# Attention sums in one PSUM bank: half-width matmuls for the left-over queries

## The chip, the cores and the metric

The kernel runs on one core of a Trainium2 chip. A core has TensorE (PE, matrix products into PSUM), VectorE (DVE), ScalarE (ACT), GpSimd (POOL), SyncE (SP, here only issuing transfers), 16 DMA engines, an on-chip memory of 128 partitions (SBUF) and the accumulator memory PSUM with eight banks of 2 KiB per partition. The metric is the device time of one execution in microseconds.

## The reference

An attention over 8 batches of 12 heads, with normalized queries and keys, followed by a feed-forward layer over all 3584 rows.

```python
batch, n_heads, seq, head_dim = (8, 12, 448, 64)
def rmsnorm(x, g):
    rms = np.sqrt(np.mean(x * x, axis=-1, keepdims=True) + 1e-06)
    return x / rms * g
q_n, k_n = (rmsnorm(q, g_q), rmsnorm(k, g_k))
scores = scale * np.matmul(q_n, k_n.transpose(0, 1, 3, 2))
scores = scores - np.max(scores, axis=-1, keepdims=True)
attn = np.exp(scores)
attn = attn / (np.sum(attn, axis=-1, keepdims=True) + 1e-09)
attn_out = np.matmul(attn, v)
...
x = attn_out.transpose(0, 2, 1, 3).reshape(B * S, H * D)      # 3584 x 768
h = x @ w_in                                                  # 768 -> 2048
relu6 = np.clip(h + 3.0, 0.0, 6.0)
out = (h * relu6 / 6.0) @ w_out                               # 2048 -> 768
```

## The kernel before

**Pairs of heads.** Two heads make a pair (48 pairs, six a batch), and one pair's 128 columns are one contraction block of the feed-forward. The 448 positions of a head are three blocks of 128 and a rest of 64 (`NT` = 3, `REST` = 64). The two rests of the keys share one 128-row block with zeros elsewhere, so that a fourth key block serves both heads at once.

**What is done for a pair `p`.** Keys, queries and values are loaded as fp32. `square` (POOL, early also ACT), `sums` (DVE) and `rstd` (two small ACT instructions) give the inverse root of the mean square; `normalize` (POOL, one instruction for keys and one for queries) writes bf16. Eight 128x128 blocks are then transposed, by PE into PSUM for the first 16 pairs (`transposes`, line 384) and by a DMA transpose afterwards; `put_q` scales the queries with the gains. `score` (line 407) multiplies keys by queries: for the three full key blocks one matmul per head, each on 64 rows of the array, the two heads' matmuls writing to two banks; for the rest block a single one of 128 rows. `expo` (line 417, ACT) writes the exponentials as bf16 tiles `eD` (both heads) or `eR` (rest block), laid out key by query.

**The weighted sums.** `weigh` (line 430) uses a window of 128 query columns of an exponential tile as weights and the value block with an added column of ones (`vaug`, 64 + 1 columns) as moving data, so that the output has queries on partitions and the denominator in its 65th column. 448 queries do not fill four windows. The exponential tiles are therefore 512 columns wide (`W4`), and columns 448 to 511 are filled once with ones by `fill_e`. In even batches the fourth window is 384 to 511; in odd batches the windows are shifted so that the 64 left-over queries stand on partitions 64 to 127, where the joint row blocks of two batches want them. Each key block gives eight matmuls of 65 columns, the rest block four of 130. The sums of a pair lie in `av`, four windows at a stride of 256 fp32, that is two banks. `divide` (lines 438 and 439, DVE) takes the reciprocal of the denominators and multiplies, giving `xn`. `x_out` (line 449, PE, first 12 pairs, then copied by `put_x`) or a DMA transpose (`x_out_dma`) turns `xn` into `xT`, the moving operand of the feed-forward.

**The feed-forward.** For each batch, `h_mm` (line 463) makes 16 groups of six matmuls with 448 columns; `relu` (line 469, ACT) and `gate` (line 474, DVE) turn each into a block of `gT`. `y_mm` (line 482) makes 16 matmuls of 384 columns for each half of an output row block, `y_copy` copies them out, `y_store` writes the rows. Weights come over POOL's DMA queue.

**PSUM.** Two double banks (`sc`, for scores), two single banks (`ps`) and the two of `av`: eight. Feed-forward groups use the single banks, `ff_banks`, and, after the last score, the double ones too.

**What sets the order.** No scheduler of a library does: the class `Plan` (lines 45 to 222) plays the kernel through at build time with estimated costs in ns and writes the instructions of every engine in the order in which its model starts them. Each `add(key, ways, deps, ...)` is a step, with the engines that can take it, its cost, and a rank. For PE, feed-forward groups (`item`) and attention steps share the engine by `share`, a credit per unit of batch progress. `PRICE` and `FIRST` weigh one engine against another, `BULK`, `LATE`, `SLACK` describe transfers, `CALM` holds the weight loads back while other transfers are queued (line 187), `NFAST` is the number of first pairs whose squares may go to ACT, and `ANY` the order in which banks are tried. At run time engines only wait for each other's semaphores; the order is fixed.

Of the kernel before, what the change touches and what calls it, by code (L numbers as in the profile page):

```python
# [44 lines left out]
class Plan:  # L45
# [3 lines left out]
    PRICE, FIRST, UNTIL = {"POOL": 0.5, "ACT": 2.0, "DVE": 1.5}, {"POOL": 0.7, "ACT": 1.5, "DVE": 0.9}, 45e3  # L49
# [122 lines left out]
    def run(self):  # L172
        now = 0.0
        while self.todo or self.row or any(self.lanes.values()):
# [8 lines left out]
            for op in self.known:  # L183
# [3 lines left out]
                if op.calm is not None and (self.backlog("SP", "ACT") > op.calm[0] or self.backlog("POOL") > op.calm[1]):  # L187
                    continue
# [37 lines left out]
def kernel(  # L226
# [48 lines left out]
    ssq_r = ring(NR, [P, 2, 8], FP32, "ssq")  # L275
    lnv_r = ring(NR, [P, 2, 8], FP32, "lnv")
    rstd_r = ring(NR, [P, 2, 8], FP32, "rstd")
# [4 lines left out]
    rden_r = ring(2, [P, 4, 2], FP32, "rden")  # L282
    xn_r = ring(NQ, [P, 4, 2 * D], BF16, "xn")
# [6 lines left out]
    unit_r = ring(2, [P, 2, 512], FP32, "sc", psum) + ring(2, [P, 1, 512], FP32, "ps", psum)  # L290
    av_ps = psum.tile([P, 4, 256], FP32, name="av")
# [7 lines left out]
    plan = Plan(share=(1.0, 1.0, 0.45, 3.0, 0.42, 6.0, 0.4))  # L299
# [57 lines left out]
    def sums(p, a, m):  # L357
        nc.vector.tensor_reduce(  # L358
            out=ssq_r[p % NR][:, a].rearrange("p a s -> p (a s)"),
            in_=sq_r[m % 2][:, a].rearrange("p a s d -> p (a s) d"), axis=mybir.AxisListType.X, op=A_ADD,  # L360
        )

    def rstd(p, a):
        nc.scalar.activation(out=lnv_r[p % NR][:, a], in_=ssq_r[p % NR][:, a], func=LN, bias=1e-6, scale=1.0 / D)
        nc.scalar.activation(out=rstd_r[p % NR][:, a], in_=lnv_r[p % NR][:, a], func=EXP, bias=0.0, scale=-0.5)  # L365

    def normalize(eng, p, a):
        eng.tensor_tensor(  # L368
            out=qkn_r[p % NQ][:, a].rearrange("p t h d -> p h t d"), in0=qk_st[:, a, p % NS],
            in1=rstd_r[p % NR][:, a].rearrange("p (h t) -> p h t", h=2).unsqueeze(3).to_broadcast([P, 2, 4, D]),  # L370
# [481 lines left out]
```

## Time and profile before

| what | value |
|---|---|
| median of 3 runs | 429.16 us (429.08 to 430.69) |
| the profiled execution | 428.99 us |
| its span, first to last instruction | 427.2 us |
| granted TensorE clock | 0.999 |
| busy: PE, ACT, DVE, POOL | 407.9, 264.7, 219.3, 213.5 us |
| first matmul | 8.83 us |
| last weighted sum (`av`) | 325.9 us |

The profile is of one execution. Its page lists busy time by engine, forty slices of the span, DMA queues, the chain of work that ended last, and groups of instructions by line and shape; the trace behind it answers for stretches and single instructions. Busy time of PE counts every matmul from its first read to its modelled end, so neighbours overlap and the busy share says little of the rate; the rate is the distance of starts. "PEld" rows are the loading of weights, which overlaps matmuls. A shape such as `64*128 64x448` is that of the weights' array part and of the moving data.

### The profile page before, as it was taken

The numbers are of one execution on the slowest core, as the hardware profiler recorded it, in microseconds if no ns is written. First come the engines' busy times: TensorE is split into PE (matmuls) and PEld (weight loads), VectorE is DVE, ScalarE is ACT, GpSimd is POOL, SyncE is SP. The second block draws the span as 40 slices with busy tenths as digits, with TensorE's granted clock in tenths as the row PEclk, the third lists the DMA queues.
The fourth block names the chain that finished last, engine by engine and source line by source line (L and its number), as shares of the span: only waits on it lengthen the run. The fifth ranks groups of instructions, "written<-read, shape, count | busy, mean of one in ns | idle before, by whom it ended". The sixth has DMA issues, their size and how long they took to land.

```text
span 427.2 us, 8968 instructions
## 1 busy us (share of the span) xinstructions
PE 407.9 (95%) x3536; PEld 232.4 (54%) x3536; DVE 219.3 (51%) x382; ACT 264.7 (62%) x490; POOL 213.5 (50%) x233
## 2 busy tenths in 40 slices
PE   1888999999999999999999999999999999999997
PEld 0555555555555455555555555555566555555565
DVE  5686867674553756556556465324344253253222
ACT  4998888778677888778776787567751142032100
POOL 6999989884594779868858377301000000000000
PEclk9999999999999999999999999999999999999999
DMA  7999998999999999999698858343202200100122
GB/s 198 233 253 217 163 226 142 237 179 198 220 243 268 194 227 185 250 226 216 133 272 170 191 130 176 61 111 76 64 12 75 75 0 38 74 2 37 73 76 74
DMA packets 125738, 64.03 MB, mean 150 GB/s; under 512 B 74736, under 2 KB 122240, under 8 KB 125696
## 3 DMA queue, kind: packets, MB, share of 16 engines
q1 hardware_dynamic: 114480, 56.72, 59.5%
q0 software_dynamic: 10528, 6.31, 11.0%
q8 instruction: 27, 0.44, 0.5%
q10 hardware_dynamic: 688, 0.43, 0.3%
q14 instruction: 15, 0.12, 0.1%
HBM read 45.61 MB, written 11.01 MB: 133 GB/s over the span
## 4 chain that ended last, share of the span: by engine, by line
PE 83%; POOL 4%; DMA 3%; ACT 3%; DVE 2%; SPq 2%; issue 2%; ACTq 0%; POOLq 0%
PE ps L482 32%; PE ps L463 29%; PE av L430 8%; PE sc L407 8%; PE sc L482 3%; DMA qk_st<-in_q_dram 2%; PE sc L463 2%; POOL sq L355 2%; ACT eD L417 1%; POOL qkn L368 1%; SPq L332 1%; DVE ssq L358 1%; DMA v_st<-in_v_dram 1%; DVE gT L474 1%; SPq L324 1%
## 5 line engine op out<-in xcount | busy, mean ns | idle before, releaser
L463 PE MATMUL ps<-xT,w_in_sb 128*128 128x448 bf16 x720 | 163.8, 353 | 1.1 <-DVE gT L474 0.9
L482 PE MATMUL ps<-w_out_sb,gT 128*128 128x384 bf16 (+1 forms) x832 | 151.7, 323 | 0.1
L417 ACT ACTIVATE eD<-sc 128x896 bf16<-128x896 f32 x144 | 127.5, 915 | 22.1 <-PE sc L407 14.2
L469 ACT ACTIVATE t_sb<-ps 128x448 f32<-128x448 f32 x120 | 65.4, 545 | 77.3 <-PE ps L463 73.6
L482 PEld LDWEIGHTS <-gT 128*128 128x128 bf16 x912 | 83.2, 98 | 55.0 <-issue 8.1
L474 DVE SCALAR_TENSOR_TENSOR gT<-t_sb,ps 128x448 bf16<-128x448 f32 x120 | 74.1, 618 | 75.2 <-ACT t_sb L469 74.7
L368 POOL TENSOR_TENSOR qkn<-qk_st,rstd 128x512 bf16<-128x512 f32 x96 | 97.9, 1043 | 24.8 <-ACT rstd L365 22.0
L463 PEld LDWEIGHTS <-w_in_sb 128*128 128x128 bf16 x768 | 68.4, 97 | 60.5 <-issue 12.8
L355 POOL TENSOR_TENSOR sq<-qk_st 128x1024 f32<-128x1024 f32 (+1 forms) x46 | 82.1, 1799 | 8.8 <-DMA qk_st<-in_q_dram 6.7
L407 PE MATMUL sc<-qkT 64*128 64x448 bf16 (+1 forms) x336 | 60.7, 359 | 4.8 <-ACT eD L417 3.4
L358 DVE TENSOR_REDUCE ssq<-sq 128x16 f32<-128x1024 f32 (+1 forms) x50 | 58.4, 1171 | 11.3 <-POOL sq L355 7.1
L430 PEld LDWEIGHTS <-eD 128*128 128x128 bf16 x1152 | 53.0, 98 | 20.4 <-issue 3.1
L335 DVE COPY y_sb<-ps 128x384 f32<-128x384 f32 (+1 forms) x45 | 24.7, 548 | 68.6 <-PE ps L482 68.5
L430 PE MATMUL av<-vaug,eD 128*128 128x65 bf16 x1152 | 58.7, 194 | 0.0
L335 POOL CAST vaug<-v_st 128x512 bf16<-128x512 f32 x32 | 19.7, 619 | 55.7 <-PE av L430 54.8
L417 ACT ACTIVATE eR<-sc 128x448 bf16<-128x448 f32 x48 | 26.1, 544 | 12.9 <-PE sc L407 12.6
L439 DVE TENSOR_TENSOR xn<-av,rden 128x512 bf16<-128x512 f32 x48 | 33.2, 691 | 1.7
L407 PEld LDWEIGHTS <-qkT 64*128 64x128 bf16 (+1 forms) x336 | 14.9, 94 | 32.9 <-issue 27.4
L438 DVE RECIPROCAL rden<-av 128x8 f32<-128x8 f32 x48 | 9.8, 205 | 27.3 <-PE av L430 26.7
L396 ACT ACTIVATE qkT<-qkT,gprime 128x448 bf16<-128x448 bf16 x32 | 21.4, 668 | 1.0 <-DMA qkT<-qkn 1.0
L430 PE MATMUL av<-vaug,eR 128*128 128x130 bf16 x192 | 19.0, 222 | 0.3 <-DVE xn L439 0.3
L430 PEld LDWEIGHTS <-eR 128*128 128x128 bf16 x192 | 14.0, 98 | 8.5 <-issue 1.9
(54 smaller groups left out, 146.7 us busy)
## 6 DMA issues: line engine op xcount, KB each, us to landing
v_st<-in_v_dram SPq DMA_DIRECT2D x24, 384.0 KB, 6.0
qk_st<-in_k_dram SPq DMA_DIRECT2D x23, 384.0 KB, 4.6
qk_st<-in_q_dram SPq DMA_DIRECT2D x23, 384.0 KB, 5.1
out_dram<-y_sb SPq DMA_DIRECT2D x23, 384.0 KB, 2.6
w_in_sb<-in_moe_w_in_dram POOLq DMA_DIRECT2D x8, 384.0 KB, 5.8
w_out_sb<-in_moe_w_out_dram POOLq DMA_DIRECT2D x4, 768.0 KB, 10.9
out_dram<-y_sb SPq DMA_DIRECT2D x9, 192.0 KB, 2.7
v_st<-in_v_dram SPq DMA_DIRECT2D x24, 64.0 KB, 5.1
```

What stands on the lines that cost most here:

```text
L335: (eng.copy if eng is nc.scalar else eng.tensor_copy)(out=out, in_=in_)
L355: eng.tensor_tensor(out=sq, in0=x, in1=x, op=A_MULT)
L358: nc.vector.tensor_reduce(out=ssq_r[p % NR][:, a].rearrange("p a s -> p (a s)"), in_=sq_r[m % 2][:, a].rearrange("p a s d -> p (a s) d"), ...
L368: eng.tensor_tensor(out=qkn_r[p % NQ][:, a].rearrange("p t h d -> p h t d"), in0=qk_st[:, a, p % NS], in1=rstd_r[p % NR][:, a].rearrange(" ...
L407: nc.tensor.matmul(out=bank(u, h)[:, 0:S], lhsT=qkT[rows, 0, i * P:(i + 1) * P], rhs=qkT[rows, 1, 0:S], start=True, stop=True,)
L417: nc.scalar.activation(out=e[..., 0:S], in_=src[..., 0:S], func=EXP, bias=0.0, scale=1.0)
L430: nc.tensor.matmul(out=out, lhsT=e_tile(p, i, h)[:, c0:c0 + P], rhs=rhs, start=first and j % 2 == 0 and h == 0, stop=last, skip_group_chec ...
L439: nc.vector.tensor_tensor(out=xn_r[p % NQ][:].rearrange("p n (h d) -> p n h d", h=2), in0=av4[:, :, :, 0:D], in1=rden[:].unsqueeze(3).to_b ...
L463: nc.tensor.matmul(out=bank(m)[:, 0:S], lhsT=w_in_sb[:, kt, f * P:(f + 1) * P], rhs=xT[:, kt, b % NX, x_slot(b)], start=(kt == 0), stop=(k ...
L469: nc.scalar.activation(out=t[:], in_=bank(m)[:, 0:S], func=RELU, bias=0.5, scale=1.0 / 6.0,)
L474: nc.vector.scalar_tensor_tensor(out=gT[:, f, (b % 2) * S:(b % 2 + 1) * S], in0=t[:], scalar=1.0, in1=bank(m)[:, 0:S], op0=A_MIN, op1=A_MULT,)
L482: nc.tensor.matmul(out=bank(m)[:, 0:n], lhsT=gT[:, f, c0:c0 + P], rhs=w_out_sb[:, f, c:c + n], start=(f == 0), stop=(f == NFT - 1),)
```

## The change: half-width sums, one bank, a third single bank

**Weighted sums.** The exponential tiles are 448 columns wide and are not padded; `fill_e` is gone. `weigh` uses windows 0 to 127, 128 to 255 and 256 to 383 in every batch, and for the fourth only the 64 queries that are left: these matmuls have 64 weight columns and write to 64 partitions, head 0 to partitions 0 to 63 and head 1 to 64 to 127, one below the other in the same 65 PSUM columns. A key block still gives eight matmuls, the rest block five instead of four. A pair's sums are 7 x 65 = 455 fp32 columns: one bank. The instructions of the changed program carry the array part 128x64 for these.

**Division and transposition.** `divide` handles seven groups of 65. For the first 12 pairs it is a reciprocal and one multiply; later it is a reciprocal, one multiply of 384 elements and two of 64 on half the partitions. `x_out` transposes three blocks of 128x128 and two of 64x64. `clear_x` sets the unused part of `xn` to zero once.

**Banks.** The bank that `av` no longer takes becomes a third `ps`; feed-forward groups and transposes rotate over three.

**The beginning.** `rstd` and `normalize` can keep their factor in a PSUM bank, and for the second array of pairs 0 and 1 (`DN`) the normalization then runs on DVE, the first staying on POOL. `finish` could serve two pairs with one `rstd`; with `MG = NPAIR` it never does.

**Numbers of the planner.** As in the diff; `NFAST` 7 becomes 6, weight loads are held back less, exponentials get a later rank.

```diff
-    PRICE, FIRST, UNTIL = {...}, {"POOL": 0.7, "ACT": 1.5, "DVE": 0.9}, 45e3
-    ISSUE, DEPART, LAND, BULK, DEPTH = 630, 1260, 1600, 0.52, 8
-    STEADY, SLACK, LATE = 60e3, 500, {"load": 2500, "turn": 2000}
+    PRICE, FIRST, UNTIL = {...}, {"POOL": 0.7, "ACT": 1.3, "DVE": 0.9}, 45e3
+    ISSUE, DEPART, LAND, BULK, DEPTH = 630, 1260, 1600, 0.58, 8
+    STEADY, SLACK, LATE = 60e3, 500, {"load": 3000, "turn": 2000}
-    UNITS = 4
+    UNITS = 5
...
-                if op.calm is not None and (self.backlog("SP", "ACT") > op.calm[0] or ...
+                if op.calm is not None and (self.backlog("SP", "ACT") > op.calm[0] + 1000 or ...
...
-    eD_r = ring(NED, [P, 2, W4], BF16, "eD")
-    eR_r = ring(NER, [P, W4], BF16, "eR")
+    eD_r = ring(NED, [P, 2, S], BF16, "eD")
+    eR_r = ring(NER, [P, S], BF16, "eR")
...
-    unit_r = ring(2, [P, 2, 512], FP32, "sc", psum) + ring(2, [P, 1, 512], FP32, "ps", psum)
-    av_ps = psum.tile([P, 4, 256], FP32, name="av")
+    unit_r = ring(2, [P, 2, 512], FP32, "sc", psum) + ring(3, [P, 1, 512], FP32, "ps", psum)
+    av_ps = psum.tile([P, 512], FP32, name="av")
...
-    plan = Plan(share=(1.0, 1.0, 0.45, 3.0, 0.42, 6.0, 0.4))
+    plan = Plan(share=(2.0, 1.0, 0.45, 3.0, 0.42, 6.0, 0.4))
...
+    def in_bank(u):
+        return bank(u)[:, 0:32].rearrange("p (n a s) -> p n a s", n=2, a=2)
+
+    def rstd(p, n, a, u=None):
+        r = slice(p % NR, p % NR + n)
+        nc.scalar.activation(out=lnv_r[:, r, a], in_=ssq_r[:, r, a], func=LN, bias=1e-6, scale=1.0 / D)
+        to = rstd_r[:, r] if u is None else in_bank(u)[:, 0:n]
+        nc.scalar.activation(out=to[:, :, a], in_=lnv_r[:, r, a], func=EXP, bias=0.0, scale=-0.5)
...
     def weigh(p, i, first, last):
         va = vaug[p % NV]
-        for j in range(4):
-            c0 = j * P if (p // HP) % 2 == 0 else (j * P - P if j else S - P)
-            for h in range(2 if i < NT else 1):
-                if i == NT:
-                    out, rhs = av_ps[:, j, 0:2 * W], va[:, NT].rearrange("p h d -> p (h d)")
-                else:
-                    out, rhs = av_ps[:, j, h * W:(h + 1) * W], va[:, i, h]
+        for j in range(NT + 1):
+            for h in range(1 if i == NT and j < NT else 2):
+                c, n = (2 * j + h) * W if j < NT else 2 * NT * W, 2 * W if i == NT and j < NT else W
                 nc.tensor.matmul(
-                    out=out, lhsT=e_tile(p, i, h)[:, c0:c0 + P], rhs=rhs,
-                    start=first and j % 2 == 0 and h == 0, stop=last, skip_group_check=True,
+                    out=av_ps[(lo, hi)[h] if j == NT else slice(0, P), c:c + n],
+                    lhsT=e_tile(p, i, h)[:, j * P:min(j * P + P, S)],
+                    rhs=va[:, i].rearrange("p h d -> p (h d)")[:, h * W:h * W + n],
+                    start=first and j == 0 and h == 0, stop=last, skip_group_check=True,
                 )
...
+        av7 = av_ps[:, 0:7 * W].rearrange("p (n d) -> p n d", n=7)
+        rden, xn, odd = rden_r[p % 2], xn_r[p % NQ], (p // HP) % 2
+        by = rden[:].unsqueeze(2).to_broadcast([P, 7, D])
+        nc.vector.reciprocal(out=rden[:].unsqueeze(2), in_=av7[:, :, D:W])
+        if p < XD:
+            out = xn.rearrange("p n (h d) -> p (n h) d", h=2)[:, 0:7]
+            nc.vector.tensor_tensor(out=out, in0=av7[:, :, 0:D], in1=by, op=A_MULT)
+            return
+        out = xn[:, odd:odd + NT].rearrange("p n (h d) -> p (n h) d", h=2)
+        nc.vector.tensor_tensor(out=out, in0=av7[:, 0:6, 0:D], in1=by[:, 0:6], op=A_MULT)
+        for h, rows in enumerate((lo, hi)):
+            out = xn[hi, 0, h * D:(h + 1) * D] if odd else xn[lo, NT, h * D:(h + 1) * D]
+            nc.vector.tensor_tensor(out=out, in0=av7[rows, 6, 0:D], in1=by[rows, 6], op=A_MULT)
...
     def x_out(p, b):
-        for i in range(4):
-            nc.tensor.transpose(bank16(b)[:, i * P:(i + 1) * P], xn_r[p % NQ][:, i], identity[:])
+        xn, odd = xn_r[p % NQ], (p // HP) % 2
+        for i in range(NT):
+            nc.tensor.transpose(bank16(b)[:, (i + odd) * P:(i + odd + 1) * P], xn[:, i], identity[:])
+        c = REST if odd else FULL
+        for rows in (lo, hi):
+            nc.tensor.transpose(bank16(b)[rows, c:c + REST], xn[rows, NT, 0:D], identity[rows, rows])
...
-    NFAST = 7
+    NFAST = 6
...
-    SC, ANY = [(0,), (1,)], [(3,), (2,), (1,), (0,)]
+    SC, ANY = [(0,), (1,)], [(2,), (3,), (4,), (1,), (0,)]
...
-    ff_banks = [(2,), (3,)]
+    ff_banks = [(2,), (3,), (4,)]
...
+    DN = ((0, 1), (1, 1))
+    MG, EACH = NPAIR, 0.5
...
-    pad = add((-5, 9), [("POOL", 1700, lambda: fill_e(G))])
+    pad = add((1, 9), [("POOL", 200, lambda: clear_x(G)), ("DVE", 200, lambda: clear_x(V))])
...
-                e = add((p, 0), [("ACT", 800 if i < NT else 440, ...
+                e = add((p, 2.5), [("ACT", 800 if i < NT else 440, ...
...
-                    div.append(add((p + 0, 0), [("DVE", 850, lambda p=p: divide(p))], [w, at(xo, p - NQ)]))
+                    div.append(add((p + 0, 0), [("DVE", 790 if p < XD else 1170, lambda p=p: divide(p))], [w, at(xo, p - NQ), pad]))
```

More of the change, by code (lines that the diff above doesn't have):

```diff
@@ L186, in run @@
                     continue
-                if op.calm is not None and (self.backlog("SP", "ACT") > op.calm[0] or self.backlog("POOL") > op.calm[1]):
+                if op.calm is not None and (self.backlog("SP", "ACT") > op.calm[0] + 1000 or self.backlog("POOL") > op.calm[1]):
                     continue
@@ L511, in ones, with clear_x @@
         eng.memset(vaug[i][0:REST, NT, 1, D:D + 1], 0.0)
-    def fill_e(eng):
-        for e in eR_r:
-            eng.memset(e[:, S:W4], 1.0)
-        for e in eD_r:
-            eng.memset(e[:, :, S:W4], 1.0)
+    def clear_x(eng):
+        eng.memset(xn_t[:, :, NT, D:2 * D], 0.0)
     def load_g(eng):
@@ L708 @@
         st = p - 2 if p < HP else p + LATER
[L709 to L734 removed]
+        if p < 2:
+            s2 = stats(p, st)
+            for a in range(2):
+                finish(p, 1, a, st, [s2[a]], (p, a) in DN)
+        elif p < MG or p not in norms:
+            n = 2 if p >= MG else 1
+            s2 = [stats(i, st)[0] for i in range(p, p + n)]
+            finish(p, n, None, st, s2, p in DN)
         if p == 0:
             mg = add((-3, 0), [("POOL", 500, make_g)], [lg])
[L737 to L739 removed]
         vc.append(add((p, 7), [("POOL", 575, lambda p=p: cast_v(G, p)),
```

92 lines of the change are left out of this document (42 added, 50 removed).

## The prediction

> **What bounds the kernel now.** I read the page first: busy shares and the chain that ended last.
>
> ```profile
> span 427.2 us, 8968 instructions
> ...
> PE 407.9 (95%) x3536; PEld 232.4 (54%) x3536; DVE 219.3 (51%) x382; ACT 264.7 (62%) x490; POOL 213.5 (50%) x233
> ...
> PE 83%; POOL 4%; DMA 3%; ACT 3%; DVE 2%; SPq 2%; issue 2%; ACTq 0%; POOLq 0%
> ```
>
> The chain is TensorE for 83% of the span. The table by stretches says where it is not (columns: stretch, its length, then busy us and instructions of PE, weight loads, DVE, ACT, POOL, then granted clock, DMA share, GB/s).
>
> ```profile
> 10.00:20.00 10.00, 8.59 (x92) 5.18 (x91) 6.32 (x13) 9.32 (x21) 9.34 (x12) 1.00 1.17 246
> 20.00:30.00 10.00, 7.90 (x112) 5.24 (x111) 7.50 (x16) 9.86 (x20) 9.59 (x12) 1.00 1.15 245
> 30.00:40.00 10.00, 8.48 (x121) 5.55 (x121) 6.75 (x14) 8.31 (x16) 9.18 (x10) 1.00 1.16 250
> 40.00:80.00 40.00, 38.47 (x408) 22.63 (x407) 29.97 (x54) 34.59 (x69) 36.84 (x37) 1.00 0.99 181
> 80.00:326.00 246.00, 245.49 (x2221) 136.37 (x2219) 128.97 (x207) 180.83 (x329) 141.75 (x137) 1.00 0.85 173
> 326.00:427.20 101.20, 98.15 (x590) 56.88 (x586) 34.31 (x59) 17.41 (x32) 0.00 (x0) 0.99 0.14 49
> ```
>
> Up to 40 us ACT and POOL are nearly full and PE has gaps; from 80 us to the last matmul PE is idle for half a microsecond, and the clock is granted in full. So the end is the time at which PE starts, plus its gaps up to 80 us, plus what its instructions cost. Busy matmuls overlap here, so that cost is read from one start to the next. The timeline of PE gives it (start, us of the merged group, engine, line, tile, shape, count):
>
> ```profile
> 202.90 0.41 PE L430 MATMUL av<-vaug,eD 128*128 128x65 bf16 x8
> 203.15 0.73 PE L463 MATMUL ps<-xT,w_in_sb 128*128 128x448 bf16 x3
> ...
> 205.77 1.30 PE L463 MATMUL ps<-xT,w_in_sb 128*128 128x448 bf16 x6
> 207.00 0.55 PE L407 MATMUL sc<-qkT 64*128 64x448 bf16 x4
> 207.48 0.40 PE L430 MATMUL av<-vaug,eR 128*128 128x130 bf16 x4
> 207.72 2.11 PE L482 MATMUL ps<-w_out_sb,gT 128*128 128x384 bf16 x12
> ```
>
> A group of eight weighted-sum matmuls takes 0.25 us (31 ns each), the four of 130 columns 0.24 (60 ns). Six full matmuls of 448 columns at 189 ns (the chain has 2.27 us for 12) are 1.13 us, but the scores behind them start after 1.23. Those scores are 64 rows high, two side by side: four take 2 x 0.19 = 0.38 us, and what follows starts after 0.48. Each change between the full array and half-height tiles costs about 0.095 us. Over all such places the starts in the trace say the same: 285 ns instead of 189 going in (42 places), 281 going out (36), two halves of one pair starting 3 to 4 ns apart.
>
> **The change part by part.** The profiled execution took 428.99 us, 1.8 more than its span; the median of the three runs is 429.16, so the sum is made against 428.99.
>
> *Weighted sums.* For each pair and key block, `weigh` issued eight matmuls of 65 columns, or four of 130. Now six of 65 (three of 130) stay at full width and two of 65 columns are half-width: 64 weight columns, output on partitions 0 to 63 or 64 to 127. Streamed columns stay the same: 24 x 65 + 4 x 130 = 2080 a pair before, and 24 x 65 + 3 x 130 + 2 x 65 = 2080 after. The gain can only be that the two half-width ones run side by side, as the half-height ones do: 192 groups x (31 - 4) = 5.2 us, bounds 0 and 5.2; I take 4.4, as the first eight of 48 pairs fall where PE has gaps.
>
> The price is the change of tile shape. In the order in which the two programs issue them, PE changes shape 168 times before and 562 times after. Of the 394 more, 372 are into and out of half-width, and some 22 come from `x_out`, whose two 64x64 transposes are new for the first 12 pairs. No half-width matmul is in the trace. The bounds are 0 (the row of a full-width matmul behind another, 31 ns with nothing on top) and 0.095 each (the row of half-height tiles). The half-height row is nearer: it is the one row in which the array is split and joined again. So 394 x 0.094 = 37.0 us. About eight pairs and seven `x_out` lie before 44 us: 8 x 8 + 7 x 2 = 78 changes, 7.3 us. By the starts, PE has 10.7 us of gaps there, behind ACT and POOL; I let 5 of the 7.3 vanish in them (bounds 2 and 7). Net +32.0.
>
> The Trainium skill, "TensorEngine Tiling (Array Packing)", section Key Properties, says that changing the tiling mode, and not merely the tile, drains TensorE, and lists 128x64 among the modes; by it the sum is as here. The trace agrees for half-height tiles (0.094 us) and cannot show the rest. The same page's Restrictions say that column tiling disables Fast Weight Load; with 64 columns / 1.2 = 53 ns ("TensorE: Matmul & The Clock Gate", section LDWEIGHTS) in place of 31, an estimate from these pages, the sum would be 192 x 22 ns = 4.2 us higher.
>
> *Division.* For the first 12 pairs DVE's multiply handles 448 elements instead of 512. For the other 36, one of 512 (691 ns) becomes one of 384 (by its slope near 560) and two of 64 (by the 8-element reciprocal, 205 ns, near 200 each): some 0.25 us more a pair. DVE is 52% busy from 80 to 326 us. The weighted sums of the next pair wait for it: they start 0.5 us or more after the division ends in nearly every pair past the twelfth (once 0.06). I count 0; without this cover 36 x 0.25 = 9.
>
> *Third single bank.* It can only remove PE gaps: 40 - 38.47 = 1.5 us between 40 and 80 us and 0.5 us up to 326. It can't make one. Bounds 0 and -2; I take -1.
>
> *The beginning.*
>
> ```profile
> 7.73 2.04 POOL L368 TENSOR_TENSOR qkn<-qk_st,rstd 128x512 bf16<-128x512 f32 x2
> ...
> 8.83 0.61 PE L384 MATMUL ps<-identity,qkn 128*128 128x128 bf16 x4 [8.83 <-POOL qkn L368]
> ...
> 9.83 0.61 PE L384 MATMUL ps<-identity,qkn 128*128 128x128 bf16 x4 [0.39 <-POOL qkn L368]
> ...
> 11.46 1.04 PE L407 MATMUL sc<-qkT 128*128 128x448 bf16 x3 [1.02 <-DVE qkT L335]
> ```
>
> POOL normalizes keys and queries one after the other, 1.02 us each, and the second four transposes wait for that. Now DVE takes the second one, at about 0.69 us (its row of 512 elements from PSUM), beside POOL's first: the transposes can end 1.0 us sooner, for pair 1 as well, and POOL, full here, loses 2 us of work. Bounds 0 and -3; I take -1.5. The eleven memsets of padding go (1.5 us of POOL up to 5.4 us); POOL then waits for `gk_t` until 6.95 anyway, and a single memset replaces them: 0.
>
> *Planner numbers* (weights of the feed-forward issued sooner, exponentials later in rank, pair 6 squared on POOL alone) act where ACT and POOL are full: 0, bounds -2 and +2. After 326 us only feed-forward runs and PE has no gap: 0.
>
> Sum: 428.99 + 32.0 - 4.4 - 1 - 1.5 = 454.1.
>
> **The rivals.** *Half-width costs nothing to change to (faster).* The halves keep all 128 rows and write to partitions of their own, where half-height tiles share their output partitions, so the 0.094 us may belong to rows alone. Against it: a change of shape is all that the half-height places have in common. Then only the changes for 64x64 tiles count, 22 x 0.094 = 2.1, 1.5 outside gaps: 428.99 + 1.5 - 4.4 - 1 - 1.5 = 423.6. The point that decides between faster and slower is 5.4 us over the 372 x 0.87 changes outside the gaps: 17 ns a change.
>
> *Half the price.* Weight loads of one shape may hide in part behind the other: 0.047 us x 372 = 17.5, less 2.5 in the gaps: 423.6 + 15 = 438.6. No row speaks for it; half-height shows the same price in both directions.
>
> *The division delays the sums.* With free shapes, a wait of PE for DVE appears at the first weighted sum of each pair past the twelfth: 0.2 to 0.25 us x 36 = 7 to 9, minus the 5.4: 431 at most, near no change. It needs the planner to have spent the half microsecond that separates them now; the row "PE av <- DVE xn" is 0.3 us in total.
>
> **How the numbers follow.** Full price 0.46, half price 0.10, free 0.38, delayed division or a cancelling mix 0.06. The likeliest gives 454, its own range is 444 (more hidden, cheaper beginning) to 460 (nothing hidden, slow weight loads). For eight in ten the range must reach over the free case too: 420 to 458. A measurement here can tell about 0.5% (2.1 us) from no change. Faster 0.38, same 0.06, slower 0.56; where faster and slower are this close, the price of one half-width change is nearly the whole question.
>
> **What would show it.** Right: in the timeline a half-width pair starts about 0.12 us after the full-width matmul before it instead of 0.03, what follows starts about 0.12 after the pair, the two halves start 4 ns apart, and "issue" appears as what weight loads of `weigh` waited for; the last weighted sum moves from 326 us to about 350, while the stretch after it keeps its 101 us. Wrong: the pair follows at 31 ns and the last weighted sum comes before 323. The beginning is right if the first scores start near 10.5 us, the division if the wait of `av` for `xn` stays under 1 us. A slower kernel with cheap pairs and a new PE gap behind DVE or ACT would make me wrong in the mechanism too.

## The result, and the profile after

The changed kernel took 464.6 us (median of four runs, 464.2 to 465.7) against 429.9 us for the kernel before in the same session (429.1 to 431.0). The ratio is 1.0809, with a 95% interval of 1.0773 to 1.0846: slower, and above the forecast of 454 and its range of 420 to 458.

| what | before | after |
|---|---|---|
| span of the profiled execution | 427.2 us | 463.9 us |
| last weighted sum (`av`) | 325.9 us | 360.4 us |
| stretch after it | 101.3 us | 103.5 us |
| first scores | 11.46 us | 11.18 us |

First the page of the kernel after (busy time, share of the span and instructions by engine, then the chain that ended last, by engine and by line):

```profile
span 463.9 us, 9117 instructions
...
PE 449.3 (97%) x3596; PEld 250.9 (54%) x3596; DVE 231.7 (50%) x455; ACT 265.7 (57%) x485; POOL 213.8 (46%) x226
...
PE 95%; DMA 2%; ACT 0%; DVE 0%; ACTq 0%; issue 0%; POOL 0%; SPq 0%; POOLq 0%
PE ps L479 34%; PE ps L498 33%; PE av L434 15%; PE sc L414 10%; PE ps L391 2%; DMA qk_st<-in_q_dram 1%; DMA v_st<-in_v_dram 1%; PE ps L462 1%; PE ps L465 0%; ACT eD L424 0%; ACTq L331 0%; DVE xn L448 0%; POOL vaug L336 0%; SPq L333 0%; ACTq L325 0%
```

The chain is now TensorE for 95% of the span, 83% before, although there are only 60 more matmuls. No other engine has taken over: "DVE xn", the division, stands at 0%. The table by stretches (length, then busy us and instructions of PE, weight loads, DVE, ACT, POOL, then granted clock, DMA share, GB/s):

```profile
10.00:20.00 10.00, 8.16 (x61) 4.30 (x61) 5.71 (x10) 8.72 (x19) 9.12 (x12) 1.00 1.17 257
20.00:30.00 10.00, 10.00 (x88) 6.06 (x87) 4.61 (x8) 7.73 (x15) 5.60 (x8) 1.00 0.91 191
30.00:40.00 10.00, 9.40 (x108) 5.53 (x108) 6.45 (x14) 7.95 (x12) 6.94 (x6) 1.00 0.96 190
40.00:80.00 40.00, 39.81 (x385) 22.45 (x384) 25.64 (x48) 31.45 (x61) 33.07 (x35) 1.00 0.91 173
80.00:326.00 246.00, 246.00 (x2053) 134.01 (x2052) 131.32 (x255) 170.05 (x311) 153.19 (x149) 1.00 0.81 172
326.00:360.00 34.00, 34.00 (x296) 19.32 (x295) 15.74 (x36) 16.78 (x27) 1.24 (x2) 1.00 0.19 48
360.00:463.90 103.90, 100.86 (x609) 58.48 (x607) 35.85 (x63) 18.47 (x34) 0.00 (x0) 1.00 0.14 49
```

From 80 to 326 us PE is never idle and the clock is granted in full, and yet it gets 2053 instructions through where the kernel before got 2221. PE does less per microsecond: a change of tile shape counts as busy in these columns. From 20 us on it is already fuller than before (10.00 instead of 7.90) with fewer instructions (88 instead of 112). The timeline of PE (start, us of the merged group, engine, line, tile; a merged row shows the shape of its first instruction):

```profile
211.84 1.30 PE L479 MATMUL ps<-xT,w_in_sb 128*128 128x448 bf16 x6
212.97 0.50 PE L434 MATMUL av<-vaug,eD 128*128 128x65 bf16 x8
213.41 0.74 PE L479 MATMUL ps<-xT,w_in_sb 128*128 128x448 bf16 x3
213.98 0.50 PE L434 MATMUL av<-vaug,eD 128*128 128x65 bf16 x8
214.42 0.93 PE L479 MATMUL ps<-xT,w_in_sb 128*128 128x448 bf16 x4
...
218.87 0.48 PE L434 MATMUL av<-vaug,eR 128*128 128x130 bf16 x5
219.28 0.74 PE L479 MATMUL ps<-xT,w_in_sb 128*128 128x448 bf16 x3
```

A group of eight now takes from 212.97 to 213.41, 0.44 us, where it took 0.25. The rest block takes 0.41 instead of 0.24. By single starts over the whole trace, the step from the last full-width matmul to the half-width pair is 124 ns instead of 30 in a group of eight (150 instead of 57 in the rest block), and the step from the second half of the pair to what follows is 150 ns instead of 33. The two halves start 3 to 4 ns apart. Added up from these usual steps, a group of eight went from 0.243 to 0.428 us and a group of the rest block from 0.228 to 0.418: 144 x 0.185 + 48 x 0.190 = 35.8 us over the kernel, about the whole loss of 34.7 (464.6 - 429.9).

### The profile page after: what moved, and what is told of

The parts are those of the page before. It is cut to its first block, busy times and chain, and to the rows that moved or that the text cites. A ratio compares the mean times of both kernels' runs of the same rounds, so it can differ in the third digit from the quotient of the medians.

```text
span 463.9 us, 9117 instructions
## 1 busy us (share of the span) xinstructions
PE 449.3 (97%) x3596; PEld 250.9 (54%) x3596; DVE 231.7 (50%) x455; ACT 265.7 (57%) x485; POOL 213.8 (46%) x226
## 4 chain that ended last, share of the span: by engine, by line
PE 95%; DMA 2%; ACT 0%; DVE 0%; ACTq 0%; issue 0%; POOL 0%; SPq 0%; POOLq 0%
PE ps L479 34%; PE ps L498 33%; PE av L434 15%; PE sc L414 10%; PE ps L391 2%; DMA qk_st<-in_q_dram 1%; DMA v_st<-in_v_dram 1%; PE ps L462 1%; PE ps L465 0%; ACT eD L424 0%; ACTq L331 0%; DVE xn L448 0%; POOL vaug L336 0%; SPq L333 0%; ACTq L325 0%
## 5 line engine op out<-in xcount | busy, mean ns | idle before, releaser
L479 PE MATMUL ps<-xT,w_in_sb 128*128 128x448 bf16 x768 | 175.7, 354 | 0.2 <-DVE xT L476 0.2
L498 PE MATMUL ps<-w_out_sb,gT 128*128 128x384 bf16 (+1 forms) x912 | 168.0, 324 | 0.0
L485 ACT ACTIVATE t_sb<-ps 128x448 f32<-128x448 f32 x128 | 69.6, 544 | 96.5 <-PE ps L479 95.0
L490 DVE SCALAR_TENSOR_TENSOR gT<-t_sb,ps 128x448 bf16<-128x448 f32 x128 | 79.2, 620 | 80.7 <-ACT t_sb L485 79.6
L498 PEld LDWEIGHTS <-gT 128*128 128x128 bf16 x912 | 82.1, 98 | 60.7 <-issue 10.8
L434 PEld LDWEIGHTS <-eD 128*128 128x128 bf16 (+1 forms) x1152 | 61.1, 101 | 31.1 <-issue 4.3
L434 PE MATMUL av<-vaug,eD 128*128 128x65 bf16 (+1 forms) x1152 | 73.9, 203 | 0.0
L445 DVE RECIPROCAL rden<-av 128x7 f32<-128x7 f32 x48 | 9.8, 203 | 39.9 <-PE av L434 39.7
L434 PE MATMUL av<-vaug,eR 128*128 128x130 bf16 (+1 forms) x240 | 24.0, 224 | 0.6 <-POOL vaug L336 0.6
L434 PEld LDWEIGHTS <-eR 128*128 128x128 bf16 (+1 forms) x240 | 16.6, 103 | 13.9 <-issue 3.5
L451 DVE TENSOR_TENSOR xn<-av,rden 128x384 bf16<-128x384 f32 x36 | 20.1, 557 | 1.2
```

The lines of the kernel that those rows point to most:

```text
L434: nc.tensor.matmul(out=av_ps[(lo, hi)[h] if j == NT else slice(0, P), c:c + n], lhsT=e_tile(p, i, h)[:, j * P:min(j * P + P, S)], rhs=va[: ...
L479: nc.tensor.matmul(out=bank(m)[:, 0:S], lhsT=w_in_sb[:, kt, f * P:(f + 1) * P], rhs=xT[:, kt, b % NX, x_slot(b)], start=(kt == 0), stop=(k ...
L485: nc.scalar.activation(out=t[:], in_=bank(m)[:, 0:S], func=RELU, bias=0.5, scale=1.0 / 6.0,)
L490: nc.vector.scalar_tensor_tensor(out=gT[:, f, (b % 2) * S:(b % 2 + 1) * S], in0=t[:], scalar=1.0, in1=bank(m)[:, 0:S], op0=A_MIN, op1=A_MULT,)
L498: nc.tensor.matmul(out=bank(m)[:, 0:n], lhsT=gT[:, f, c0:c0 + P], rhs=w_out_sb[:, f, c:c + n], start=(f == 0), stop=(f == NFT - 1),)
```

## Experiments

### Is it the half-width matmuls alone?

My theory was that the change of shape is the price. The rivals were that the banks, the planner's numbers or the division had a hand in it. In `e1_full_width` everything of the change stays, but the left-over queries are weighed with 128 weight columns into the same 65 PSUM columns, so that both heads' rows add up there. The left-over sums are therefore not those of the reference. Array work, banks and order are otherwise those of after.

```diff
-                    out=av_ps[(lo, hi)[h] if j == NT else slice(0, P), c:c + n],
-                    lhsT=e_tile(p, i, h)[:, j * P:min(j * P + P, S)],
+                    out=av_ps[:, c:c + n],
+                    lhsT=e_tile(p, i, h)[:, min(j * P, S - P):min(j * P + P, S)],
```

> The changed kernel with the left-over queries summed by full-width matmuls of the last 128 query columns (both heads into the same 65 PSUM columns, so that the sums of the left-over queries are not the reference's); everything else as changed, the order of work too. Shape changes of PE fall from 562 to 190. If the half-width matmuls are the whole loss: 192 groups x 0.187 us (what a group takes from start to start now, less what it took before) = 35.9 us less than 464.6, so 428.7, and last weighted sum near 325 us. If the loss lies elsewhere (third bank, division, planner's order): 445 or more.

Measured: 428.45 us, ratio to before 0.9965 (0.9941 to 0.9989). After minus this is 464.6 - 428.45 = 36.2 us, against 35.8 by the starts. The timeline of this kernel has the group of eight back at 0.25 us (203.61 to 203.86):

```profile
203.61 0.41 PE L434 MATMUL av<-vaug,eD 128*128 128x65 bf16 x8
203.86 0.35 PE L479 MATMUL ps<-xT,w_in_sb 128*128 128x448 bf16 x1
```

The two programs issue their 3596 matmuls in the same order, so that single starts can be compared one by one. After is 0.3 us ahead at the first scores, lags by 5.5 us at its 44 us (24 half-width groups), by 21.5 at 200 us (108 groups) and by 37.9 at the end (192 groups), 0.20 us a group. That is 10 ns a group more than the 0.185 to 0.190 above: the first full-width matmul behind a half-width pair is followed late as well, after 200 ns instead of 189 (448 columns) or 173 instead of 163 (384 columns). With these 192 x 10 ns = 1.9 us the account is 37.7 us, against 37.8 between the two profiled spans (463.9 - 426.1) and 36.2 between the medians, whose runs spread over more than a microsecond.

So the loss is the half-width matmuls, and none of it is hidden behind other engines in this order.

The opposite test, `e4_before_half`, puts half-width matmuls into the kernel before, in the three full key blocks only (144 groups); banks, numbers and order stay. The rest block still writes its wide window and the full blocks' sums of head 1 lie on other partitions, so the left-over sums are again not the reference's.

```diff
+                rest = i < NT and j == (NT if (p // HP) % 2 == 0 else 0)
+                if rest:
+                    out = av_ps[(lo, hi)[h], j, h * W:(h + 1) * W]
+                cols = slice(FULL, S) if rest else slice(c0, c0 + P)
                 nc.tensor.matmul(
-                    out=out, lhsT=e_tile(p, i, h)[:, c0:c0 + P], rhs=rhs,
+                    out=out, lhsT=e_tile(p, i, h)[:, cols], rhs=rhs,
```

> The kernel before, in its own order, with one part of the change alone: for the three full key blocks the left-over window is summed by two half-width matmuls on 64 partitions each (head 1's, or head 0's in odd batches, land on the padding rows, so that these left-over sums are not the reference's). 144 groups x 0.185 us = 26.6 us more than before, 456, if the half-width matmuls act wherever they stand; at 40 us and earlier the gaps of PE could hide up to 4 of them, 452. If they need the changed order or banks to hurt: 432 or less.

Measured: 451.13 us against 430.26, ratio 1.047 (1.0425 to 1.0515), that is +20.9 us; 144 x 0.185 is 26.6. In the order of before some 6 us of it did vanish (3.4 us if the two profiled spans are compared: 450.4 - 427.2 = 23.2). The price per group is the same here: 201.80 to 202.23 in its timeline is 0.43 us. PE's gaps took up 3 us of it, if a gap is what a step from start to start is longer than the median of its kind, where that is over 20 ns: they sum to 0.3 us instead of 2.5 between 40 and 80 us, and to 0.3 instead of 1.2 between 80 and 326 us. Before 40 us they stay within 0.2 us of the kernel before.

```profile
201.80 0.50 PE L434 MATMUL av<-vaug,eD 128*128 128x65 bf16 x8
202.23 0.36 PE L407 MATMUL sc<-qkT 128*128 128x448 bf16 x1
```

### By the matmul, or by the change?

If each half-width matmul were slow in itself, the price would follow their number, 384. If the change of shape is what costs, it follows the number of entries, 192. `e2_gather` keeps all 384 but issues the half-width pairs of all four key blocks together behind the pair's last key block: 48 entries instead of 192. It computes the same as after.

```diff
-        for j in range(NT + 1):
+        for i, j in [(i, j) for j in range(NT)] + [(x, NT) for x in seen if last]:
...
-                w = add((p + 1, 1), [("PE", 264 if i < NT else 240,
-                                      lambda p=p, i=i, k=k, last=last: weigh(p, i, k == 0, last))],
+                order.setdefault(p, []).append(i)
+                w = add((p + 1, 1), [("PE", (198 if i < NT else 180) + 440 * last,
+                                      lambda p=p, i=i, k=k, last=last: weigh(p, i, k == 0, last, order[p]))],
```

> The changed kernel with the half-width pairs of all four key blocks of a pair of heads issued together after its last key block: as many half-width matmuls (384), 288 shape changes instead of 562. If each change costs 0.094 us whatever is in between: 274 x 0.094 = 25.8 us less, 439. If the price hangs on each half-width matmul (slow weights), not on the change: no gain, 460 or more. Inside a group, pairs follow each other at 57 ns if the two halves stream one after the other, at 31 ns if they stream side by side; with 31 ns the time is 434.

Measured: 432.74 us, ratio 1.0063 (1.0034 to 1.0092). The same 384 matmuls cost 4.3 us over full width instead of 36.2. Their timeline (the first row of eight is six full-width ones and the first pair):

```profile
223.73 0.50 PE L434 MATMUL av<-vaug,eD 128*128 128x65 bf16 x8
224.06 0.20 PE L434 MATMUL av<-vaug,eR 128*64 128x65 bf16 x2
224.09 0.23 PE L434 MATMUL av<-vaug,eD 128*64 128x65 bf16 x4
224.26 0.99 PE L498 MATMUL ps<-w_out_sb,gT 128*128 128x384 bf16 x5
```

By the starts behind these rows, the four pairs begin at 224.007, 224.059, 224.095 and 224.124: 52 ns from the first to the second, then 36 and 29. So a pair takes as long as one full-width matmul of 65 columns: the two halves do run side by side and save about 29 ns a pair. What follows starts 130 ns after the last half here (224.258 behind 224.128), and 125 to 130 ns in 46 of the 48 groups. The account is 48 entries x (94 in + 94 out + 25 once inside) = 10.2 us, less 192 x 29 ns = 5.6: +4.6, measured +4.3. I had expected more than was measured, because I had not counted that gain in full.

### Why 150 ns on the way out?

94 ns for the change and 31 for streaming 65 columns make 125, so 26 ns are left over. Two explanations were tried. If the two halves ran one after the other at the end, leaving out one of them would save it. `e3_one_half` leaves out head 1's half-width matmul in the three full key blocks.

```diff
-            for h in range(1 if i == NT and j < NT else 2):
+            for h in range(1 if (i == NT) == (j < NT) else 2):
```

> The changed kernel without head 1's half-width matmul in the three full key blocks (those sums are left out). What follows the half-width group now starts 0.151 us after the pair. If the halves stream one after the other, a single one is followed after 0.124 (0.151 less 27 ns), and the time falls by 144 x 0.027 = 3.9 us to 461. If they stream side by side and leaving half-width is simply dearer (0.120), or its weights load slowly, 0.151 stays and the time too, 464 to 466.

Measured in a single run: 463.97 us, no different from after (464.2 to 465.7). The step from the half-width matmul to what follows is still 150 ns, and the group of seven takes 0.43 us:

```profile
212.46 0.50 PE L434 MATMUL av<-vaug,eD 128*128 128x65 bf16 x7
212.89 0.93 PE L479 MATMUL ps<-xT,w_in_sb 128*128 128x448 bf16 x4
```

If the streaming of both halves counted, more columns would count twice. `e6_wide` streams 122 instead of 65 columns in every half-width matmul (the added columns lie in unused PSUM, and the left-over sums are not the reference's).

```diff
+                o = h * W
+                if j == NT:
+                    o, n = 0, 512 - c
...
-                    rhs=va[:, i].rearrange("p h d -> p (h d)")[:, h * W:h * W + n],
+                    rhs=va[:, i].rearrange("p h d -> p (h d)")[:, o:o + n],
```

> The changed kernel with 122 instead of 65 moving columns in every half-width matmul (head 1's then has head 0's columns, so that the left-over sums are not the reference's). 57 columns more take 24 ns of streaming. If the two halves run side by side and what follows waits for a late weight load besides, the next start moves from 0.151 to 0.175 us after the pair, and the time grows by 192 x 0.024 = 4.6 us to 469. If they stream one after the other: 0.198 us and 474.

Measured in a single run: 468.55 us, 4.0 more than the median of after. The way out went from 151 to 173 ns, 22 more, about one stream of 57 columns (189 ns for 448 columns is 0.42 ns each, so 24), not two. 192 x 22 ns = 4.2 us.

```profile
214.02 0.52 PE L437 MATMUL av<-vaug,eD 128*128 128x65 bf16 x8
214.47 0.74 PE L482 MATMUL ps<-xT,w_in_sb 128*128 128x448 bf16 x3
```

So the halves overlap, and the 26 ns are neither the second half nor its columns. `e2_gather` places them: they come once per entry, right behind the first half-width pair (52 ns to the second pair instead of about 31), whatever follows. The groups by shape hint at the weights. After (weight loads "PEld", then matmuls; busy us, mean ns of one):

```profile
L434 PE MATMUL av<-vaug,eD 128*128 128x65 bf16 x864 | 51.9, 197 | 0.0
L434 PEld LDWEIGHTS <-eD 128*128 128x128 bf16 x864 | 45.2, 99 | 23.0 <-issue 4.3
L434 PE MATMUL av<-vaug,eD 128*64 128x65 bf16 x288 | 32.3, 221 | 0.0
L434 PEld LDWEIGHTS <-eD 128*64 128x64 bf16 x288 | 16.0, 107 | 8.1
```

And gathered:

```profile
L434 PE MATMUL av<-vaug,eD 128*64 128x65 bf16 x288 | 13.8, 199 | 0.0
L434 PEld LDWEIGHTS <-eD 128*64 128x64 bf16 x288 | 9.1, 112 | 1.0
```

The weight-load records of 64 columns are longer, 107 ns where 128 columns have 99. Their length alone is no price: loads of 128 columns support a start every 30 ns, and the gathered loads have 108 to 112 ns although their pairs start every 29 to 36 ns. The loads of the gathered group show what differs at the entry:

```profile
224.00 0.11 PEld L434 LDWEIGHTS <-eD 128*64 128x64 bf16 x2
224.03 0.11 PEld L434 LDWEIGHTS <-eR 128*64 128x64 bf16 x2
224.06 0.15 PEld L434 LDWEIGHTS <-eD 128*64 128x64 bf16 x4
```

The first pair of loads starts at 224.005 and its matmuls at 224.007, 2 ns later. The second pair of loads starts at 224.034, 25 ns ahead of its matmuls at 224.059. The first matmul in the new shape also has a longer record, 218 ns against 197 for those that follow it. The same is seen, smaller, behind every change back to full width: 363 against 352 ns for 448 columns, with the 10 ns that the next one is late. Over the whole traces of before, after and `e2_gather` the first matmul behind a change starts 2 to 4 ns (median) after its load, at any shape, while nearly all others have theirs 26 ns or more ahead. So the first matmul behind a change has no load ahead of it. A weight load that is slower at half width and exposed once per entry fits the 26 ns; no run isolates it, so their reason remains an inference.

### The rest of the change

`e1_full_width` against before is only -1.8 us, with a third bank, a shorter beginning and other planner numbers in it. These were taken apart. `e5_full_two_banks` is `e1_full_width` with two single banks (left-over sums as there).

```diff
-    SC, ANY = [(0,), (1,)], [(2,), (3,), (4,), (1,), (0,)]
+    SC, ANY = [(0,), (1,)], [(2,), (3,), (1,), (0,)]
...
-    ff_banks = [(2,), (3,), (4,)]
+    ff_banks = [(2,), (3,)]
...
-                           want=any_of((2,), (3,), (4,)) if kt == 0 else None, cell=cell))
+                           want=any_of((2,), (3,)) if kt == 0 else None, cell=cell))
```

> The full-width version of the changed kernel (both heads' left-over sums into the same columns, not the reference's) without the third single bank: feed-forward and transposes use two. If the third bank is what made that version 1.8 us faster than the kernel before: 430 to 431. If it removes nothing, since PE had no gap left there: 428.5 within 1.

`e8_rest_only` takes sums, division, transposes and banks from before and keeps the beginning (`DN`) and the planner's numbers. Its edit is the reverse of the change's, in its core:

```diff
-    unit_r = ring(2, [P, 2, 512], FP32, "sc", psum) + ring(3, [P, 1, 512], FP32, "ps", psum)
-    av_ps = psum.tile([P, 512], FP32, name="av")
+    unit_r = ring(2, [P, 2, 512], FP32, "sc", psum) + ring(2, [P, 1, 512], FP32, "ps", psum)
+    av_ps = psum.tile([P, 4, 256], FP32, name="av")
...
-    UNITS = 5
+    UNITS = 4
```

> The changed kernel with its sums, division, transposition and banks put back as they were before (128-wide padded windows, two banks for the sums, two single banks): what is left of the change is the normalization on DVE at the beginning and the planner's numbers. If these two made the full-width version faster: 426 to 428.5, since also the 22 shape changes of the 64x64 transposes (2.1 us) are gone. If the third bank did it: 430 to 431.

`e9_dn_only` is `e8_rest_only` with the planner's numbers of before, `e12_full_old_numbers` is `e1_full_width` with them (left-over sums as there), by this edit (`e9_dn_only` also tries the two single banks in the order of before):

```diff
-    PRICE, FIRST, UNTIL = {...}, {"POOL": 0.7, "ACT": 1.3, "DVE": 0.9}, 45e3
-    ISSUE, DEPART, LAND, BULK, DEPTH = 630, 1260, 1600, 0.58, 8
-    STEADY, SLACK, LATE = 60e3, 500, {"load": 3000, "turn": 2000}
+    PRICE, FIRST, UNTIL = {...}, {"POOL": 0.7, "ACT": 1.5, "DVE": 0.9}, 45e3
+    ISSUE, DEPART, LAND, BULK, DEPTH = 630, 1260, 1600, 0.52, 8
+    STEADY, SLACK, LATE = 60e3, 500, {"load": 2500, "turn": 2000}
...
-                if op.calm is not None and (self.backlog("SP", "ACT") > op.calm[0] + 1000 or ...
+                if op.calm is not None and (self.backlog("SP", "ACT") > op.calm[0] or ...
...
-    plan = Plan(share=(2.0, 1.0, 0.45, 3.0, 0.42, 6.0, 0.4))
+    plan = Plan(share=(1.0, 1.0, 0.45, 3.0, 0.42, 6.0, 0.4))
...
-    NFAST = 6
+    NFAST = 7
...
-                e = add((p, 2.5), [("ACT", 800 if i < NT else 440, ...
+                e = add((p, 0), [("ACT", 800 if i < NT else 440, ...
```

> As the last one, with the planner's numbers of before as well: the normalization of pairs 0 and 1 on DVE is the only part of the change. In the changed kernel the first scores start 0.28 us sooner than before, so 0.3 us less than the kernel before, 430.0; if POOL's lighter load carries through the first 40 us, up to 2 us less, 428.3.

> The full-width version with three single banks (both heads' left-over sums into the same columns, not the reference's) and the planner's numbers of before. With the new numbers it took 428.5, with the new numbers and two banks 437.4. If the third bank is worth its 9 us under any order: 421 to 424. If it only pays for gaps that the new numbers open when two banks must do: 427 to 430, as with the new numbers.

`e10_numbers_only` is `e8_rest_only` without `DN`: the planner's numbers, with the order in which banks are tried, and nothing else.

```diff
-    DN = ((0, 1), (1, 1))
+    DN = ()
```

> The changed kernel's planner numbers alone: sums, division, transposition and banks as before, and no normalization on DVE. With it the time was 437.3, and the normalization on DVE alone cost 1.6 us. If the numbers open the gaps: 435 to 437. If it takes both: near 431.

Measured (median us, and the ratio to before with its interval):

| | two single banks | three single banks |
|---|---|---|
| numbers of before | `e9`: 431.86, 1.0045 (1.0026 to 1.0064) | `e12`: 430.0, 1.0003 (0.9985 to 1.0022) |
| numbers of after | `e8`: 437.34, 1.017 (1.0133 to 1.0206); `e5`: 437.37, 1.0159 (1.0139 to 1.018) | `e1`: 428.45, 0.9965 (0.9941 to 0.9989) |

All five have `DN`; `e10_numbers_only`, without it, took 436.36, 1.0166 (1.013 to 1.0203), so with two single banks the numbers alone cost 6.2 us. With the numbers of before, bank and one-bank sums together bring 431.86 - 430.0 = 1.9 us; with those of after, the bank alone brings 437.37 - 428.45 = 8.9. With three single banks the numbers bring 430.0 - 428.45 = 1.6. `e5`, `e8` and `e9` took longer than anything that had been expected of them. The stretches from 40 us (columns as above) show where. Three banks and the numbers of after, `e1_full_width`:

```profile
40.00:80.00 40.00, 40.00 (x436) 22.99 (x434) 30.29 (x55) 34.26 (x66) 36.79 (x36) 1.00 1.06 205
80.00:326.00 246.00, 246.00 (x2267) 137.34 (x2265) 140.94 (x283) 180.23 (x329) 145.60 (x143) 1.00 0.86 172
```

Two banks, `e5_full_two_banks`:

```profile
40.00:80.00 40.00, 38.83 (x413) 21.25 (x411) 28.80 (x55) 32.39 (x62) 35.68 (x37) 1.00 1.00 192
80.00:326.00 246.00, 242.67 (x2222) 134.87 (x2222) 137.70 (x276) 183.28 (x335) 143.81 (x140) 1.00 0.83 172
```

PE is idle for 1.2 + 3.3 us where with three banks it is idle for none, and part of it is named in PE's waits of `e5_full_two_banks` (us in total, times, longest), rows that `e1_full_width` lacks:

```profile
PE ps L479 <- DVE gT L490: 1.3, 5, 0.4
PE sc L414 <- ACT eR L424: 0.7, 2, 0.4
...
PE ps L498 <- DVE gT L490: 0.4, 2, 0.2
```

In the first and the last of these rows a feed-forward group waits until the gate has read the bank that it is to use. Busy matmuls overlap, so these columns show only part of the gaps. By the starts (gaps as for `e4_before_half`), `e5_full_two_banks` has 2.2 us more of them than `e1_full_width` before 40 us, 1.5 more between 40 and 80 and 6.0 more up to 326, together 9.7 of the 9.9 us between the two spans (436.0 - 426.1). In the same way `e10_numbers_only` has 2.4, 0.4 and 3.6 us more gaps than the kernel before, 6.4 in all. So the new numbers open gaps with two banks and not with three. Which number does it was not tried.

Last, whether a gathered version could gain. `e11_gather_full_x` is `e2_gather` with full 128x128 transposes for the first 12 pairs as before, for which these pairs are also divided in the three pieces of the later ones; `e14_gather_old_numbers` is that with the planner's numbers of before. Both compute the same as after.

```diff
-        for i in range(NT):
-            nc.tensor.transpose(bank16(b)[:, (i + odd) * P:(i + odd + 1) * P], xn[:, i], identity[:])
-        c = REST if odd else FULL
-        for rows in (lo, hi):
-            nc.tensor.transpose(bank16(b)[rows, c:c + REST], xn[rows, NT, 0:D], identity[rows, rows])
+        for i in range(4):
+            nc.tensor.transpose(bank16(b)[:, i * P:(i + 1) * P], xn[:, i], identity[:])
...
-        eng.memset(xn_t[:, :, NT, D:2 * D], 0.0)
+        eng.memset(xn_t[:], 0.0)
```

> Half-width pairs gathered after the last key block, and in addition the first 12 pairs transposed by four full 128x128 transposes as before, instead of three and two of 64x64. 25 shape changes fewer: 2.3 us less than 432.7, so 430.4, level with the kernel before. If the 64x64 transposes fell into gaps of PE: 432 to 433.

> Half-width pairs gathered after the last key block, full transposes, three single banks, and the planner's numbers of before. If the third bank helps under any order, 48 entries into half-width (4.6 us in all) are paid for: 425 to 429, faster than both kernels. If the new numbers suit three banks: 431 to 434.

Measured: 432.27 us, 1.0071 (1.0042 to 1.0101), and 438.1, 1.0199 (1.0173 to 1.0225). The first is level with `e2_gather` (432.74), so that a gain from leaving out the 64x64 tiles of `x_out` is not shown. The second is above both ranges that were expected of it: the numbers of before fit this order worse by 5.8 us, and the reason is open. No version with the reference's sums was faster than the kernel before.

## Why the prediction was wrong in size

The forecast went the right way (slower, with a chance of 0.56) for the reason given: PE pays for each change into and out of half-width tiles, and its last weighted sum moves. The shape change itself was right. Two terms of the sum were mis-sized: the price of a half-width group and the part of it that gaps of PE would hide.

**The price of a half-width group was mis-sized.** The step "394 x 0.094 = 37.0 us" took 94 ns each way from the half-height row. In and out that was right: 124 - 30 = 94 going in, and 125 to 130 less 31, so 94 to 99, going out of a gathered group. What it lacked is the 26 ns behind the first half-width pair, 192 x 26 ns = 5.0 us, and the 10 ns behind the first full-width matmul after it, 1.9 us. The half-height row has such late steps too: in the profile of before the second pair of scores behind a change starts after 200 ns instead of 189, and so does the matmul after the first full-width one. The prediction read the two steps at the change and not the next one. The Trainium skill's "TensorEngine Tiling (Array Packing)", section Key Properties, says that a change of tiling mode drains TensorE, and the trace agrees for half-width, with those 94 ns. The Restrictions of that page of the Trainium skill say that column tiling disables Fast Weight Load. The estimate made from that, 22 ns a group, is near the measured 26, though its cause was only inferred; taken for every pair it does not hold, since gathered pairs start every 29 to 36 ns.

**The gain from halves side by side held.** It was taken as 4.4 us, with 5.2 as the bound; the 29 ns of a pair make 192 x 29 ns = 5.6.

**"I let 5 of the 7.3 vanish in them" failed.** The gaps before 40 us hid nothing. By the starts PE's gaps there are 10.7 us before, 10.8 in `e1_full_width` and 12.2 after, and at its 44 us after lags `e1_full_width` by 5.5 us, with 24 groups done (24 x 0.195 = 4.7). The likely reason is that the chain through the first pairs runs through PE itself: a slower PE delays what the other engines wait for, and the gaps move along with it. In the order of before, by `e4_before_half`, 3 to 6 us did vanish, but in PE's gaps behind 40 us; the changed order has almost none there.

**The beginning: -1.5 was too much.** POOL and DVE do normalize side by side, and the last of the first eight transposes ends at 9.63 us instead of 10.44. The first scores start at 11.18, 0.28 us sooner, not 1.0, and even this is no more than executions differ by: they start at 10.8 to 11.5 us in the traces of the kernels with `DN` (11.51 in `e1_full_width`), at 11.0 to 11.5 in the three without. The timeline of after:

```profile
8.60 1.03 PE L391 MATMUL ps<-identity,qkn 128*128 128x128 bf16 x8 [8.60 <-POOL qkn L375]
...
9.12 0.69 DVE L359 TENSOR_REDUCE ssq<-sq 128x8 f32<-128x512 f32 x1 [1.13 <-ACT sq L354]
...
9.75 0.45 DVE L405 TENSOR_SCALAR qkT<-ps,gprime 128x448 bf16<-128x448 bf16 x1
...
10.12 0.68 DVE L359 TENSOR_REDUCE ssq<-sq 128x8 f32<-128x512 f32 x1
...
10.71 0.41 DVE L336 COPY qkT<-ps 128x512 bf16<-128x512 bf16 x1
...
11.18 1.04 PE L414 MATMUL sc<-qkT 128*128 128x448 bf16 x3 [1.55 <-DVE qkT L336]
```

The copy of the keys, at 10.71, waits in DVE's queue behind pair 1's `sums` at 10.12, and the scores wait for that copy. I followed POOL and PE and did not look at what stood in DVE's queue. Over the whole run `DN` alone even costs 1.6 us (`e9_dn_only`, 1.0045 of before); why is open.

**Third bank -1, numbers 0: right only in one order.** Bank first and numbers second, they bring 1.9 (with the one-bank sums) and 1.6 us, both inside the bounds. Numbers first and bank second, they cost 6.2 and bring 8.9, both far outside. "It can only remove PE gaps" was read against the gaps of before, though the new order makes its own when two banks must do. Both together (`e9` to `e1`) bring 3.4, inside the two bounds added up; as the same numbers cost 6 with two banks, this is in part luck.

**The division was hidden, as said.** PE's waits of after contain no row of `av` for `xn`:

```profile
PE ps L391 <- POOL qkn L375: 8.6, 1, 8.6
PE sc L414 <- DVE qkT L336: 1.6, 1, 1.6
PE av L434 <- POOL vaug L336: 0.6, 1, 0.6
PE sc L414 <- ACT eD L424: 0.5, 2, 0.3
PE ps L479 <- DVE xT L476: 0.2, 1, 0.2
```

"Free" and "half price" fell with the first group of the timeline. The sum of the delayed-division rival was wrong by itself: 423.6 plus 7 to 9 is 431 to 433, not "431 at most". The sign "issue" did not show either: weight loads of `weigh` waited for it 27 times, 7.8 us in all, against 18 times and 5.0 before, and not in 192 groups. "The stretch after it keeps its 101 us" was off by 2.2: it is 103.4 in `e1_full_width` too (426.1 - 322.7), so that is the order, with 609 matmuls left from 360 us instead of 590 from 326, and not the shapes.

Put together: 429.9 + 35.8 for the half-width groups - 1.8 for all the rest (`e1_full_width`) = 463.9, and 465.8 with the 1.9 for the first full-width matmuls; measured 464.6 (464.2 to 465.7). Against the forecast, 10.5 us short: 5.0 for the late step behind the first pair, 1.9 for the one behind the first full-width matmul, 5.0 for gaps that hid nothing, 0.9 from the base (429.9 instead of 428.99), -1.2 for the larger overlap, and -1.1 of rests that are no larger than the spread of the runs.

## What to carry to other kernels

Count the places where PE changes its tile shape before counting the work that a smaller tile saves: here a 64-column matmul pair saved 29 ns and its entry and exit cost some 220 (94 + 94 + 26 + 10), so by these numbers it would pay only when about eight such pairs stand together; four were tried and did not. Gaps of an engine in a latency-bound beginning are no cover for more work on that same engine, if the engine is itself a link of the chain. A resource such as a bank, and the numbers that order the work around it, should be measured as a pair: here the numbers alone cost 6 us, the bank with the one-bank sums alone brought 2, and all of them together brought 3.4 (431.86 - 428.45).

## What was not expected of the hardware

- Changing between the full array and half-width tiles costs 94 ns each way, the same as for half-height tiles, although the rows and the moving data stay the same. Once per entry about 26 ns come on top behind the first pair, and 10 ns behind the first full-width matmul after it. The first matmul in a new shape starts 2 to 4 ns after its own weight load; nearly all others have theirs 26 ns or more ahead.
- Two half-width matmuls on opposite halves of the columns start 3 to 4 ns apart and run side by side: 57 more columns in both lengthened the pair by 22 ns, one stream.
- The weight-load records of 64 columns are longer than those of 128 (107 against 99 ns, mean of the rows shown), and neither length is the distance at which such loads can follow one another (29 to 36 ns in the gathered pairs, 30 ns at full width).
